# Raising VectorE's softmax bits in place: two passes per group of three score tiles instead of three, and 512-column GpSimd instructions

## The chip, the cores and the metric

The kernel runs on one core of one Trainium2 chip. The metric is the device time of one execution in microseconds (us). Five engines work side by side, each through its own instructions in order: TensorE (PE in the profile; PEld are its weight loads), VectorE (DVE), ScalarE (ACT), GpSimd (POOL) and SyncE (SP), which here only issues transfers. Times come from unprofiled runs; where the time goes is read from one profiled execution.

## The reference

Two attention blocks read the same x (2048 x 512, bfloat16; 32 heads of 16) and are mixed by a gate per row:

```python
x = A_x
g = _sigmoid((x * gate_w).sum(-1, keepdims=True))
a = _A_ref(x, A_wqkv, A_wo)      # full attention: softmax(q k^T / 4) v over all 2048 keys, 32 heads
b = _B_ref(x, B_wqkv, B_wo)      # each row attends to 8 rows: itself and 2, 4, ..., 14 rows back
return g * a + (1 - g) * b
```

Block A is the bulk: 32 heads x 2048 x 2048 exponentials. Block B has 8 scores per row and head.

## The kernel before

**Block A.** The 2048 queries are cut into 4 chunks of 512, the heads into 8 groups of four; the 32 pairs of chunk and head group are the *periods*. In a period there are 64 score tiles of 128 keys x 512 queries (16 key tiles x 4 heads). Most go this way: TensorE computes scores into one of two PSUM rings (three tiles and two tiles in turn), ScalarE takes one exponential of the whole ring (`pT<-ring`), and TensorE multiplies the result with the values (`vp_all`) into the period's accumulator.

**VectorE's groups.** Some score tiles (`n_dve`: 3 to 9 in the first eight periods, 12 in each later one, 339 in all) bypass ScalarE. They come in groups of `NGR` = 3 tiles, so there are 113 groups. `d_set` (L1220) lays out a group: TensorE computes each tile's scores (`dq`), and `p1` on VectorE turns them into a 16-bit integer, scale times score plus a constant, whose bits read as bfloat16 approximate the exponential. To make this better, the same bits are also used raised by 1, 2 and 3 times `STEP` = 32, and the four versions (steps 0 to 3, `NV` = 4) are multiplied with the values under four weights (`vp_all`, and `vd_all`, which holds the values times `WEIGHTS`) and added up in the accumulator. The raised copies are made by `sh` (L1263): three VectorE passes per group, each from the group's buffer `dt` into a buffer of its own, `pd`. A pass reads 1536 elements per partition as six runs of 256 and writes three rows of 512 that lie `ROW` = 514 apart. The matmuls of a step are `dpv` (L1276): three matmuls, one per tile. From period `LATE0` = 8 on, the weights of block A are no longer needed and two of the three `dt` buffers lie in their memory (`wkv`); there are three `pd` buffers (`NPD`).

**Block B.** The 16 tiles of 128 rows of block B run beside it (`b_tile`, L882): projections on TensorE, evacuated by VectorE and written to DRAM; SyncE loads the shifted rows back (`ksh`, `vsh`); GpSimd multiplies, adds up and normalises (`prod`, `av`, `lg`), adds the two last parts into `obb`, and TensorE transposes that for the output projection (`fin`). Most of GpSimd's instructions work on `HB` = 256 columns, so a row of 512 takes two. Partial sums of `av` are made by transfers that GpSimd issues (`av_sum`), for the last two tiles by GpSimd itself. GpSimd also normalises block A's periods (`po2a`, `po2b`).

**Order.** Nothing in the order is left to the chip. Every piece of work is an `op` with an engine, an estimated duration (`parts`), a due time and dependencies; `list_schedule` (L175) simulates the engines and writes down, for each engine, the order in which its instructions are issued. Resources such as buffers and PSUM banks are tokens. A part of a duration that is marked as shared (`True` in `parts`, as in `GP` for GpSimd and `SB` for two kinds of VectorE passes) takes its turn on one common `port` in that simulation. The three `sh` passes are not marked as shared. Due times of block B come from `b_start` and `b_space` (us from one tile to the next); those of the groups from `tn`, the planned time of the score set beside which a tile was placed: the raises at tn + 1.5 + 2(m - 1), their matmuls at tn + 4.5 + 2m.

Of the kernel before, what the change touches and what calls it, by code (L numbers as in the profile page):

```python
# [22 lines left out]
    b_space=(44.0,) * 4 + (47.0,) * 4 + (49.0,) * 8,  # L23
# [16 lines left out]
ROW = QW + 2  # L40
# [3 lines left out]
NPD = 3  # L44
NDE = 1
NDL = 3
# [5 lines left out]
def _ap(base, dims):  # L52
    return bass.AP(tensor=base.tensor, offset=base.offset, ap=[list(d) for d in dims])
# [47 lines left out]
POOL_G, NPG = (), 1  # L101
# [5 lines left out]
SB = lambda n: [(True, 0.065 + n / 3840.0)]  # L107
TT = lambda n: [(True, 0.075 + n / 960.0)]
# [9 lines left out]
P1D, SHD, PO1D = -100.0, 2.0, 300.0  # L118
# [183 lines left out]
def kernel(  # L302
# [75 lines left out]
    def mm_k(out, c, i, rhs, start, stop):  # L378
        for j in range(4):
            w = wkv[:, c, (4 * i + j) * DH:(4 * i + j + 2) * DH] if j < 3 else wk3[:, c, i, :, :].rearrange("p e d -> p (e d)")  # L380
            mm(out[32 * j:32 * j + 32, :], w, rhs, start, stop, tile_position=(0, 32 * j))
# [77 lines left out]
    wkv = const.tile([128, DC, 2 * D], BF16, name="wkv")  # L459
    wq = const.tile([128, DC, D], BF16, name="wq")  # L460
    wq2 = const.tile([128, DC, 8, 2, DH], BF16, name="wq2")
    q_scr = tc.dram_tile([NG * NC // 2 * 16, DH * QW], BF16, name="q_scr")
    wk3 = const.tile([128, DC, NG, 2, DH], BF16, name="wk3")
# [25 lines left out]
    dt_a = const.tile([128, NDE * NGR * QW], BF16, name="dt_a")  # L489
    pd_a = const.tile([128, (NPD + NPG) * NGR * ROW], BF16, name="pd_a")  # L490
    wkv_l = wkv[:].rearrange("p c n -> p (c n)")
    dt_bufs = [dt_a[:, k_ * NGR * QW:(k_ + 1) * NGR * QW] for k_ in range(NDE)]
    dt_bufs += [wkv_l[:, k_ * NGR * QW:(k_ + 1) * NGR * QW] for k_ in range(NDL - NDE)]
    pd_bufs = [pd_a[:, k_ * NGR * ROW:(k_ + 1) * NGR * ROW].rearrange("p (q n) -> p q n", q=NGR) for k_ in range(NPD + NPG)]
# [58 lines left out]
    def load_w(part):  # L553
        def s():
            out = wkv[:, :, (part - 1) * D:part * D] if part else wq[:]
            SP.dma_start(out=out, in_=a_w3[:, :, part * D:(part + 1) * D])
        return s
# [16 lines left out]
    xtok = [tok("gat", NGA) if sc < NGA else tok("pd", NPD) for sc in range(NC)]  # L574
# [13 lines left out]
    def k3(E, i0, i1):  # L588
        def s():
            wk = wkv[:, :, 0:D].rearrange("p c (i j d) -> p c i j d", i=NG, j=4)  # L590
            for e, j in ((0, 3), (1, 0)):
                E.tensor_copy(out=wk3[:, :, i0:i1, e, :], in_=wk[:, :, i0:i1, j, :])
        return s
# [113 lines left out]
    def v_proj(h0, h1, tb, TB, tag, dl, rel=0.0):  # L707
# [4 lines left out]
        def mk(half):  # L712
            def s():
                if half == 0:
                    st["pv"] = misc_ps([128, TB, n], tag=tag)
                for tt in range(half * TB // 2, (half + 1) * TB // 2):
                    t = tb + tt
                    for c in range(DC):
                        mm(st["pv"][:, tt, :], xT[:, c, t * 128:(t + 1) * 128],
                           wkv[:, c, D + h0 * DH:D + h1 * DH], c == 0, c == DC - 1)  # L720
            return s
# [158 lines left out]
    HB = D // 2  # L880

    def b_tile(t):  # L882
# [195 lines left out]
        for g_, (hf, wp) in enumerate(halves):  # L1078
            ps_ = mulp(logits_mul, hf, wp) + [logits_add(hf, wp, *x) for x in adds] + [logits_out(hf, wp)]
            srcs = [None] * nm + [1, 3] + list(range(nm + 1, nm + na - 1))  # L1080
            lgs.append([(g_, k_, p_, srcs[k_], ([lk[hf], qa] if k_ == 0 else [])) for k_, p_ in enumerate(ps_)])
        lseq = lgs[0][:nm]
        for g_ in range(len(halves)):
            nxt = lgs[g_ + 1][:nm] if g_ + 1 < len(halves) else []
            ad = lgs[g_][nm:]
            lseq += ad[:3] + nxt[:2] + ad[3:] + nxt[2:]
# [28 lines left out]
        b = op("pool", 0.0, av_last(0), tb + 43, deps=[a1], alloc=[tbb], use=[tav], name=f"B{t}", parts=GP("ff", HB))  # L1115
        a1 = op("pool", 0.0, av_last(HB), tb + 43, deps=[a1], after=[b], use=[tav, tbb], name=f"B{t}", parts=GP("ff", HB))
# [99 lines left out]
    wkv_users = [o for o in ops if o.eng == "pe" and o.name.startswith(("kp", "vp"))]  # L1216
    d_st, d_last, d_sh = {}, [None, None], []
    d_count, d_ends, d_sg = [0, 0, 0, 0], [], []

    def d_set(pi, gi, t, j, qk_, tn):  # L1220
# [5 lines left out]
        if first:  # L1226
            slot = d_count[0] % NDL if late else d_count[2] % NDE
            d_count[0] += late
            d_count[2] += not late
            d_st[key] = dict(dt=dt_bufs[slot], td=tok("dtl", NDL) if late else tok("dt", NDE), js=[], ts=[], p1=[])  # L1230
# [17 lines left out]
        if first and late and d_count[0] <= NDL:  # L1248
            deps += wkv_users + d_ends[-NV * NDE:]
# [10 lines left out]
        def on_pool(m):  # L1260
            return m == NV - 1 and gi in POOL_G

        def sh(m, pb):  # L1263
            def s():
                o_, i_ = pb.bitcast(U16)[:, :, 0:QW], g["dt"].bitcast(U16)
                i_ = _ap(i_, [list(i_.ap[0]), [QW // 2, 2 * NGR], [1, QW // 2]])
                (G if on_pool(m) else V).tensor_scalar(out=o_, in0=i_, scalar1=STEP * m, scalar2=None, op0=ALU.add)
            return s

        def pv(m, pb):  # L1270
            def s():
                for n1, (t_, j_) in enumerate(zip(g["ts"], g["js"])):
                    pv_mm(pi, t_, j_, pb[:, n1, 0:QW], vd_all[:, m - 1, t_ - (NT - NTD)] if m else vp_all[:, t_])
            return s

        def dpv(m, pb, deps, use, dl):  # L1276
            b = op("pe", 0.0, pv(m, pb), dl, mode="c", js=g["js"], full=1, deps=deps + [o_t0[pi]] + vs,
                   use=[use, acc_tok[pi]], name=f"dpv{pi}")
            o_pv[pi].append(b)
            d_ends.append(b)  # L1280
        dpv(0, g["dt"].rearrange("p (q n) -> p q n", q=NGR), list(g["p1"]), g["td"], tn + 4.5)
        for m in range(1, NV):
            if on_pool(m):
                pb = pd_bufs[NPD + d_count[3] % NPG]
                d_count[3] += 1
                tp = tok("pg", NPG)
                a = op("pool", 0.0, sh(m, pb), GFIRST, deps=list(g["p1"]), alloc=[tp], use=[g["td"]], name=f"sg{pi}",
                       after=d_sg[-1:], parts=GP("one", NGR * QW))
                d_sg.append(a)
            else:  # L1290
                pb = pd_bufs[d_count[1] % NPD]
                d_count[1] += 1
                tp = tok("pd", NPD)
                a = op("dve", 0.0, sh(m, pb), tn + 1.5 + SHD * (m - 1), deps=list(g["p1"]), alloc=[tp], use=[g["td"]],
                       lat=0.065 + NGR * QW / 1920.0 + SH_LAT, after=d_sh[-1:],
                       parts=[(False, 0.065 + NGR * QW / 1920.0)], name=f"sh{pi}")
                d_sh.append(a)
            dpv(m, pb, [a], tp, tn + 4.5 + SHD * m)
# [200 lines left out]
```

## Time and profile before

| what | us |
|---|---|
| three runs: lowest, median, highest | 814.36, 819.31, 820.49 |
| the profiled execution's own time | 815.66 |
| its span, first to last instruction | 813.9 |
| ScalarE busy | 785.7 |
| first exponential starts, last one ends | 19.58, 805.1 |
| VectorE's raising passes, 339 in all | 175.3 + 135.3 |
| GpSimd busy | 633.8 |
| last `obb` ends, its transposes start | 775.5, 790.43 |

The span in 40 slices of about 20 us (tenths of a slice that an engine is busy):

```profile
PE   8999999999999998999889999989989999898996
...
DVE  5646776897887999989989899997988899898887
ACT  2999999999999999999999999999999999999995
POOL 3098969799899999999997794989769419899910
```

A group line of the profile gives line, engine, operation, output <- input, shapes and count, then busy time in us and the mean duration of one in ns, then the idle time of the engine just before these instructions and what ended it. A line of a timeline gives start, duration, engine, what it is and how many are merged. The line L364 is the helper through which VectorE, ScalarE, GpSimd and SyncE issue everything, L373 the same for TensorE, so groups are told apart by tile names: `pd_a<-dt_a` and `pd_a<-wkv` are the raising passes, `dt_a<-misc_ps` and `wkv<-misc_ps` the `p1` passes.

### The profile page before, as it was taken

The page shows a single profiled execution, that of the slowest core. Times are in us where ns is not written, and L with a number is a line of the kernel's source. Part 1 is how long each engine was busy: PE and PEld are TensorE (multiplying, and loading weights), DVE is VectorE, ACT ScalarE, POOL GpSimd, SP SyncE. Part 2 cuts the span into 40 slices and gives each one's busy share as a digit, 9 for nine tenths or more (in the row PEclk, how much of TensorE's full clock was granted, in tenths as well). Part 3 has the DMA queues.
Part 4 walks back from the last instruction along what each step waited for, and adds up shares of the span by engine and source line. Part 5 has one row for each costly group of instructions (what it writes and reads, how often), then busy time and mean ns, then how long its engine had stood idle before and what let it go on. Part 6 is the DMA issues. An engine that isn't in the chain of part 4 may idle for free.

```text
span 813.9 us, 18012 instructions
## 1 busy us (share of the span) xinstructions
PE 751.9 (92%) x6962; PEld 246.2 (30%) x7018; DVE 690.2 (85%) x1080; ACT 785.7 (97%) x706; POOL 633.8 (78%) x1058
## 2 busy tenths in 40 slices
PE   8999999999999998999889999989989999898996
PEld 4333334324222222222222222323222222222322
DVE  5646776897887999989989899997988899898887
ACT  2999999999999999999999999999999999999995
POOL 3098969799899999999997794989769419899910
PEclk9999999999999999999999999999999999999998
DMA  7503071533544344443524407162440521522000
GB/s 261 143 2 118 2 172 50 135 86 100 132 118 112 95 114 131 103 127 93 149 55 119 126 17 171 45 162 54 91 125 12 124 92 49 147 59 72 1 2 27
DMA packets 58886, 77.22 MB, mean 95 GB/s; under 512 B 3744, under 2 KB 50848, under 8 KB 58800
## 3 DMA queue, kind: packets, MB, share of 16 engines
q1 hardware_dynamic: 52752, 54.05, 21.5%
q0 software_dynamic: 6048, 22.02, 14.6%
q8 instruction: 55, 0.90, 0.5%
q14 instruction: 31, 0.25, 0.1%
HBM read 43.78 MB, written 10.26 MB: 66 GB/s over the span
## 4 chain that ended last, share of the span: by engine, by line
ACT 46%; PE 28%; issue 18%; POOL 4%; DVE 3%; DMA 1%; SPq 0%; DVEq 0%; ACTq 0%
ACT pT L364 46%; PE misc_ps L373 19%; PE ring L373 8%; POOL prod L364 2%; POOL av L364 1%; DMA xld<-in_A_x_dram 1%; DVE kt_all L364 1%; ACT lg L364 1%; DVE pd_a L364 1%; PE pxt L622 0%; DVE wkv L364 0%; DVE osb L364 0%; POOL lg L364 0%; POOL obb L364 0%; DVE accT L364 0%
## 5 line engine op out<-in xcount | busy, mean ns | idle before, releaser
L364 ACT ACTIVATE pT<-ring 128x1536 bf16<-128x1536 f32 (+1 forms) x684 | 778.6, 1319 | 10.3 <-PE ring L373 9.8
L373 PE MATMUL ring<-qt,kt_all 32*128 32x512 bf16 x1709 | 270.4, 382 | 46.1 <-ACT pT L364 36.7
L364 POOL TENSOR_TENSOR prod<-ksh,qb 128x256 f32<-128x256 bf16 x256 | 175.8, 745 | 65.2 <-DMA ksh<-kv_scr 32.8
L373 PE MATMUL misc_ps<-pT,vp_all 128*17 128x512 bf16 (+1 forms) x1709 | 208.6, 383 | 0.1
L373 PEld LDWEIGHTS <-kt_all 32*128 32x128 bf16 x2048 | 88.4, 91 | 299.7 <-issue 290.4
L364 DVE TENSOR_SCALAR pd_a<-wkv 128x1536 uint16<-128x1536 uint16 x192 | 175.3, 941 | 1.7 <-PE misc_ps L373 0.6
L364 POOL TENSOR_TENSOR prod<-prod 128x256 f32<-128x256 f32 (+1 forms) x256 | 167.1, 668 | 5.8
L364 DVE TENSOR_SCALAR wkv<-misc_ps 128x512 uint16<-128x512 f32 x192 | 129.2, 683 | 27.9 <-PE misc_ps L373 23.1
L373 PE MATMUL misc_ps<-z 128*32 128x512 bf16 x421 | 138.9, 386 | 1.6 <-DVE z L364 1.6
L364 DVE TENSOR_SCALAR pd_a<-dt_a 128x1536 uint16<-128x1536 uint16 x147 | 135.3, 944 | 1.0
L373 PE MATMUL misc_ps<-pd_a,vd_all 128*17 128x512 bf16 x1017 | 131.3, 381 | 0.2
L373 PE MATMUL misc_ps<-qt,kt_all 32*128 32x512 bf16 x339 | 125.2, 380 | 2.4 <-DVE wkv L364 0.7
L364 DVE TENSOR_SCALAR dt_a<-misc_ps 128x512 uint16<-128x512 f32 x147 | 99.1, 685 | 18.3 <-PE misc_ps L373 16.9
L364 POOL TENSOR_TENSOR prod<-vsh,lg 128x256 f32<-128x256 bf16 x128 | 81.7, 739 | 0.0
L364 POOL TENSOR_TENSOR av<-vsh,lg 128x256 f32<-128x256 bf16 x128 | 79.6, 657 | 0.0
L373 PEld LDWEIGHTS <-vp_all 128*17 128x17 bf16 (+1 forms) x2048 | 54.7, 88 | 80.1 <-issue 66.2
L373 PE MATMUL misc_ps<-bw,xT 128*128 128x512 bf16 x164 | 50.8, 384 | 2.6 <-issue 1.1
L373 PEld LDWEIGHTS <-z 128*32 128x32 bf16 x421 | 37.0, 96 | 50.7 <-issue 28.1
L373 PEld LDWEIGHTS <-vd_all 128*17 128x17 bf16 x1017 | 35.1, 88 | 47.6 <-issue 38.0
L373 PEld LDWEIGHTS <-xT 128*128 128x128 bf16 x576 | 30.2, 99 | 33.4 <-issue 29.2
L364 POOL DMA_DIRECT2D av<-av x14 | 12.3, 882 | 33.3 <-DMA av<-prod 33.3
L373 PE MATMUL misc_ps<-xT,wkv 128*32 128x512 bf16 x384 | 37.9, 382 | 0.0
(89 smaller groups left out, 584.2 us busy)
## 6 DMA issues: line engine op xcount, KB each, us to landing
ksh<-kv_scr SPq DMA_DIRECT2D x32, 512.0 KB
vsh<-kv_scr SPq DMA_DIRECT2D x32, 512.0 KB
av<-prod POOLq DMA_DIRECT2D x28, 512.0 KB, 5.8
av<-av POOLq DMA_DIRECT2D x14, 512.0 KB, 5.0
kv_scr<-kvs SPq DMA_DIRECT2D x16, 256.0 KB
qt<-q_scr SPq DMA_DIRECT2D x30, 128.0 KB
out_dram<-osb SPq DMA_DIRECT2D x16, 128.0 KB
q_scr<-qs SPq DMA_DIRECT2D x15, 128.0 KB
```

The source lines that it names most:

```text
L364: return chain_on(key, f(*a, **k))
L373: return chain(nc.tensor.matmul(out, lhsT=lhsT, rhs=rhs, start=start, stop=stop, **kw))
```

## The change

A group's buffer becomes 3072 elements wide (`ROWB` = 2 x 3 x 512). `p1` fills its first half as before. Then there are two passes, both in place and over one contiguous run, instead of three into buffers of their own: `raise1` writes the first half plus `STEP` into the second half (1536 elements), and `raise2` adds 2 x `STEP` to the whole buffer (3072 elements). Steps 0 and 1 are multiplied between the two passes, steps 2 and 3 after the second, which therefore waits for the matmuls of steps 0 and 1.

In the simulation the two passes are marked as shared (`PT`). The `pd` buffers go. There are two wide buffers (`NDT`) in the first eight periods and two more (`NCB`) from period 8 on, in the memory of A's weights: K weights, V weights, `wq2` and `wk3` now lie in one tile `wall` of 2 x 3072 elements. `HB` becomes 512: GpSimd's multiplies and the first level of its additions work on 512 columns, and `obb` is written by one instruction. Block B's tiles are due at closer intervals (`b_space`). An option to make raised copies on GpSimd, unused before (`POOL_G` was empty), is removed.

```diff
-    b_space=(44.0,) * 4 + (47.0,) * 4 + (49.0,) * 8,
+    b_space=(43.0,) * 4 + (45.0,) * 4 + (47.0,) * 8,
...
-ROW = QW + 2
-NPD = 3
-NDE = 1
-NDL = 3
+NDT = 2
+NCB = 2
+ROWB = 2 * NGR * QW
...
+PT = lambda n: [(True, 0.1 + n / 3840.0)]
...
-P1D, SHD, PO1D = -100.0, 2.0, 300.0
+P1D, SH1, SH2, PO1D = -100.0, 1.5, 4.0, 300.0
+DP = (3.0, 3.5, 6.0, 6.5)
...
+    wall = const.tile([128, NCB * ROWB], BF16, name="wall")
+    wkw, wvw = (wall[:, k_ * DC * D:(k_ + 1) * DC * D].rearrange("p (c n) -> p c n", c=DC) for k_ in range(2))
...
+    pd_a = const.tile([128, NDT * ROWB], BF16, name="pd_a")
+    cb_bufs = [b_[:, k_ * ROWB:(k_ + 1) * ROWB] for b_, n_ in ((pd_a, NDT), (wall, NCB)) for k_ in range(n_)]
...
-    HB = D // 2
+    HB = D
...
-            lseq += ad[:3] + nxt[:2] + ad[3:] + nxt[2:]
+            lseq += ad[:1] + nxt[:1] + ad[1:2] + nxt[1:] + ad[2:]
...
-        b = op("pool", 0.0, av_last(0), tb + 43, deps=[a1], alloc=[tbb], use=[tav], name=f"B{t}", parts=GP("ff", HB))
-        a1 = op("pool", 0.0, av_last(HB), tb + 43, deps=[a1], after=[b], use=[tav, tbb], name=f"B{t}", parts=GP("ff", HB))
+        a1 = op("pool", 0.0, av_last(0), tb + 43, deps=[a1], alloc=[tbb], use=[tav], name=f"B{t}", parts=GP("ff", HB))
...
-    wkv_users = [o for o in ops if o.eng == "pe" and o.name.startswith(("kp", "vp"))]
+    wkv_users = [o for o in ops if o.eng == "pe" and (o.name.startswith(("kp", "vp")) or o.name in ("qp0", "qp1"))]
...
+        n_w = NGR * QW
+        flat = g["dt"].bitcast(U16)
+
+        def raise1():
+            V.tensor_scalar(out=flat[:, n_w:2 * n_w], in0=flat[:, 0:n_w], scalar1=STEP, scalar2=None, op0=ALU.add)
+
+        def raise2():
+            V.tensor_scalar(out=flat, in0=flat, scalar1=2 * STEP, scalar2=None, op0=ALU.add)
+
+        def pv(m):
...
+                    c0 = (m % 2 * NGR + n1) * QW
+                    pv_mm(pi, t_, j_, g["dt"][:, c0:c0 + QW], vd_all[:, m - 1, t_ - (NT - NTD)] if m else vp_all[:, t_])
...
+        a = op("dve", 0.0, raise1, tn + SH1, deps=list(g["p1"]), use=[g["td"]], after=d_sh[-1:], lat=0.0,
+               parts=PT(n_w), name=f"sh{pi}")
+        d_sh.append(a)
+        a.lat = a.occ + LAT["dve"] + SH_LAT
+        b = [dpv(0, list(g["p1"]), tn + DP[0]), dpv(1, [a], tn + DP[1])]
+        a = op("dve", 0.0, raise2, tn + SH2, deps=b, use=[g["td"]], after=d_sh[-1:], lat=0.0, parts=PT(2 * n_w),
+               name=f"sh{pi}")
+        d_sh.append(a)
+        a.lat = a.occ + LAT["dve"] + SH_LAT
+        dpv(2, [a], tn + DP[2])
+        dpv(3, [a], tn + DP[3])
```

The three removed `sh` passes with their `dpv` matmuls, and the old buffers, stand in the kernel before (L1260 to L1298 and L489 to L494).

## The prediction

> **What bounds the kernel now.** I read the page's busy times and costliest groups first, then busy time by stretch, then ScalarE's waits.
>
> ```profile
> PE 751.9 (92%) x6962; PEld 246.2 (30%) x7018; DVE 690.2 (85%) x1080; ACT 785.7 (97%) x706; POOL 633.8 (78%) x1058
> ...
> L364 ACT ACTIVATE pT<-ring 128x1536 bf16<-128x1536 f32 (+1 forms) x684 | 778.6, 1319 | 10.3 <-PE ring L373 9.8
> ...
> L364 DVE TENSOR_SCALAR pd_a<-wkv 128x1536 uint16<-128x1536 uint16 x192 | 175.3, 941 | 1.7 <-PE misc_ps L373 0.6
> ```
> ```profile
> 200.00:400.00 200.00, 187.73 (x1607) 57.42 (x1623) 183.76 (x274) 199.11 (x180) 187.84 (x316) 1.00 0.46 115
> 400.00:700.00 300.00, 278.52 (x2426) 84.19 (x2441) 272.86 (x400) 300.00 (x271) 227.75 (x385) 1.00 0.37 94
> ```
> ```profile
> ACT pT L364 <- PE ring L373: 9.8, 11, 5.1
> ```
>
> The stretches list PE, weight loads, DVE, ACT, POOL, clock, DMA. ScalarE's exponentials set the end: from the first (19.58 us) to the end of the last (805.1) ScalarE is idle only 10.3 - 5.1 = 5.2 us (the 5.1 lies ahead of the first). The change leaves all 684 alone, so it can win only those 5.2 us, what little hides between the records, and the tail of 8.8 us. In 400 to 700 us 265 of ScalarE's 271 instructions are exponentials: 132.5 pairs (five score tiles each), 2.264 us a pair; the fastest pairs of the timeline start 2.235 apart. It can lose wherever it makes TensorE late for a ring. VectorE (92% in 200 to 400) and TensorE (94%) have little room, and GpSimd (94%) none while it catches up.
>
> The next rows show a raise's new partner, GpSimd. Fills of kt_all and the mask of qa are the passes of before that read one even, contiguous run from SBUF to SBUF, as the raises will; today's raising pass splits its output into three rows.
>
> ```profile
> 72.56 1.28 DVE L364 TENSOR_SCALAR kt_all<-kt_all,rowc,negk 128x2048 bf16<-128x2048 bf16 x1
> ```
> ```profile
> 72.63 1.75 POOL L364 TENSOR_TENSOR prod<-ksh,qb 128x256 f32<-128x256 bf16 x2
> ```
> ```profile
> 208.44 0.80 DVE L364 TENSOR_SCALAR kt_all<-kt_all,rowc,negk 128x2048 bf16<-128x2048 bf16 x1
> ```
> ```profile
> 152.07 2.89 DVE L364 TENSOR_SCALAR kt_all<-kt_all,rowc,negk 128x2048 bf16<-128x2048 bf16 x1
> ```
> ```profile
> L364 DVE TENSOR_SCALAR qa<-qs x15: 282/446/1175, 22.2 to 731.4; 128x256 uint32<-128x256 uint32 x15
> ...
> L364 DVE TENSOR_SCALAR pd_a<-dt_a x147: 886/944/955, 35.1 to 797.7; 128x1536 uint16<-128x1536 uint16 x147
> ```
>
> The fill takes 0.80 us with GpSimd idle (208.44) and 1.28 beside it (72.56), where two GpSimd multiplies took 1.75 us; elsewhere two such take 1.29 to 1.30. So each lost about 0.46 us to the other. At 152.07 the fill stood through a run of four multiplies, 2.09 us. Today's raise (886 to 955 ns) takes no notice of GpSimd.
>
> **The raises.** There are 339/3 = 113 groups. Removed: three passes each, 113 x 2.67 us (three in a row take 2.67 in the timeline at 180.43). Added: one pass over 1536 and one over 3072 elements. The fills alone give (0.803 - 0.407)/(2048 - 512) = 0.258 ns per element; the fixed part is 0.944 - 1536 x 0.52 = 0.145 us for an immediate operand, 0.275 for the fills' per-partition ones. That makes 0.54 + 0.94 = 1.48 us a group (at most 1.74). Taken: 1.5, as the raise has an immediate. To it come two waits for GpSimd. From 39.8 us on, 21 fills and masks took 0.32 us longer than alone on average, beside instructions of 256 columns (0.63 us from start to start). With 512 columns an instruction lasts some 1.11 us, so I scale the wait to 0.55; bounds 0 and 1.1. A group costs VectorE 1.5 + 1.1 = 2.6 us: as good as the 2.67 of now. VectorE gains nothing.
>
> **GpSimd.** Joined into 512 columns: 128 pairs of K products, 128 of V, 64 of additions, 16 of obb, 12 of the last tiles' sums: 348. A row of 128 columns takes 427 ns and one of 256 748, so 0.11 us is fixed; the timeline's pitches make it 0.14. At 0.125, 348 x 0.125 = 43 us go, 2.7 per tile of B. Against this a pass costs GpSimd 0.46/2048 per element: 0.35 + 0.69 = 1.04 us a group where they meet. Tiles 3 to 7 of B ended (obb) at 259.4 and 417.0: 39.4 us each with GpSimd 94% busy, its rate flat out. A period has 64 - 12 = 52 exponentials' tiles, 52/5 x 2.264 = 23.6 us for four groups, 5.9 a group. So a tile takes (39.4 - 2.7)/(1 - 1.04/5.9) = 44.6 us, and the last obb, 12 tiles after the fourth, ends at 259.4 + 12 x 44.6 = 795 instead of 775.5. Its transposes stand at 790.43 and their chain (evacuation, output matmuls, a copy) ends at 797.7, 11 us before the final addition at 808.72: obb may come as late as 801. Cost: 0, covered by 6 us; every us beyond is lost.
>
> [...]
>
> **Raises into TensorE.** Pairing each pass with its matmuls in the timeline, half of them start within 0.7 us of the pass's end, a quarter within 0.4; half the exponentials start within 0.37 us of their last ring matmul's end, of which 0.11 can't be saved. So a raise that GpSimd holds a microsecond longer than the written order assumes blocks TensorE's queue, where the next ring stands. What it costs isn't in the trace; the nearest rows are the nine fills and masks held over 0.3 us (39.77, 72.56, 112.40, 122.23, 152.07, 210.62, 312.34, 434.69, 684.20). Within 4 us behind them ScalarE is idle 0.23 (before 42.65), 0.43 (113.25) and 0.23 (316.09): 0.89/9 = 0.10 us each. Of 226 raises I take 60% held over 0.3 us (0.81 of 1.11 us of an instruction, at nine tenths and somewhat less for the short ones): 226 x 0.6 x 0.10 = 13.6 us. Bounds: 0, if the order has room; 34, if half of them wait 0.55 us against a cover of 0.25.
>
> New in VectorE's queue: the second raise waits for the matmuls of step 0 and 1, and behind it stand the evacuations of the next scores, for whose banks TensorE waits. Today all three passes need only the finished scores. Cover: VectorE's idle time, 16 of 200 us, 0.5 us a group. Taken at 0.
>
> **The rest.** The tail ends today with six raises in 5.24 us (799.71), ahead of the last matmuls; two groups without GpSimd take 3.0. But the last exponential ends at 805.13, so -0.5 at most; taken. Weights in one tile: the same transfers in longer runs, 0; if they were slower, the first exponential would move by as much. Raising in place holds a buffer until the fourth step's matmul; two early and four late buffers stand against 5.9 us a group: 0. Earlier due times for B move its loads up in SP's queue, but GpSimd works in order and lags its due times: 0; covered by its 32.8 us of waits for ksh.
>
> **The sum.** The profiled execution took 815.66 us, 1.76 over its span; the three runs lie 1.3 below to 4.8 above (median 819.31). 815.66 + 13.6 - 0.5 = 828.8, and something for GpSimd's thin cover: 830, slower. Its own range is 828 to 842.
>
> **Rivals.** *No change:* the written order has room. For it: the fill at 152.07 stood 2.09 us too long and ScalarE ran on (four exponentials in 4.99 us from 153.16). Against: fills have no TensorE waiter at hand. 815.66 + 0 to 10: 820. Here belongs the case that the raises don't run at the fill's rate: at 0.52 ns, 0.94 + 1.74 = 2.68 us a group and no meeting with GpSimd, so no change either.
> *Faster:* early groups (ScalarE's idle lies before 320 us) find VectorE freer, as GpSimd is idler there; its 5.2 us go, half of the (2.264 - 2.235) x 341 = 10 us between pairs not owed to B's 16 exponentials (about 5), and the tail's 0.5: 815.66 - 8 = 808. It decides if the waits stay under (2.67 - 1.5)/2 = 0.58 us. Against: 0.55 expected.
> *GpSimd becomes the bound:* it decides above (801 - 259.4)/12 = 45.1 us a tile, half a us over my value. At 1.3 us lost per group a tile takes 47.1, the last obb comes at 824.6, 24 late: 839. If passes hold GpSimd for their whole 1.48 us, 49.0, 46 late: 862. For: 94% busy in 200 to 400. Against: the 0.46.
>
> **Chances.** Forecast 0.38, GpSimd 0.14, no change 0.38, faster 0.10. One per cent is about what a measurement here can tell from none: 811.1 to 827.5 around 819.31. So faster 0.10, same 0.38, slower 0.52. The range 811 to 848 leaves out the faster case and about two thirds of the GpSimd one.
>
> **What would show it.** Raises near 0.54 and 0.94 us with GpSimd idle and about 0.5 more beside it; GpSimd's products at 1.1 us, some 0.35 to 0.7 longer beside raises; ScalarE idle 15 to 20 us, behind TensorE's ring, late in the span too. No further idle time would refute the forecast; a last obb after 801 speaks for GpSimd; raises without waits for the faster case.

## The result, and the profile after

The changed kernel took 843.76 us (median of 4 runs, 839.46 to 849.45), the kernel before 817.77 beside it: a ratio of 1.033 (95% interval 1.030 to 1.037), so about 26 us slower. That is inside the forecast's range (811 to 848) and just above its own range (828 to 842); the direction was right, the size too small.

The profiled execution took 844.3 us with a span of 842.5. The page's busy times, the clock in 40 slices and three group lines:

```profile
PE 763.5 (91%) x6947; PEld 243.6 (29%) x7000; DVE 668.4 (79%) x967; ACT 789.7 (94%) x706; POOL 669.4 (79%) x710
...
PEclk9999999998999899999999999999999999999998
...
L364 ACT ACTIVATE pT<-ring 128x1536 bf16<-128x1536 f32 (+1 forms) x684 | 782.0, 1289 | 35.2 <-PE ring L373 28.2
...
L364 DVE TENSOR_SCALAR pd_a<-pd_a 128x1536 uint16<-128x1536 uint16 (+1 forms) x130 | 153.4, 1180 | 15.3 <-PE misc_ps L373 14.2
...
L364 DVE TENSOR_SCALAR wall<-wall 128x1536 uint16<-128x1536 uint16 x96 | 121.5, 1271 | 16.8 <-PE misc_ps L373 16.2
```

The column that moved is ScalarE's idle time: 35.2 us ahead of the same 684 exponentials (10.3 before). The first exponential starts at 19.54 us (19.58 before) and the last ends at 833.99 (805.13), with 8.54 us behind it (8.76): nothing came in ahead of the stream, 0.2 us was won behind it, and the whole loss lies in it. Added up from the start of one activation to that of the next, less the shortest such distance for its shape, ScalarE is 45.0 us late in this execution and was 16.2 late before: 28.8 us more. Some 11 us of that fall between 200 and 300 us and 17 between 300 and 700; ahead of 200 us the two kernels are as late as each other, and behind 700 they differ by 1 us. The two raises take 153.4 + 121.5 = 274.9 us, where the three passes took 310.6.

Busy time by stretch (PE, weight loads, DVE, ACT, POOL, granted clock, DMA) and ScalarE's waits (total, times, longest):

```profile
200.00:400.00 200.00, 178.07 (x1458) 51.59 (x1470) 163.20 (x213) 188.57 (x168) 168.90 (x178) 0.97 0.40 102
400.00:700.00 300.00, 272.07 (x2307) 80.14 (x2320) 253.03 (x336) 288.02 (x258) 269.94 (x282) 0.99 0.36 92
```
```profile
ACT pT L364 <- PE ring L373: 28.2, 36, 5.1
...
ACT pT L364 <- PE misc_ps L373: 5.7, 4, 2.2
```

ScalarE was busy for all of 400 to 700 before; now 12 us are missing there, and no other engine is full: TensorE 272 of 300, VectorE 253, GpSimd 270. Engines with room and a late stream mean waits in a row, not a new bound. TensorE's waits name the first of them (in the kernel before, this view gave `wkv` 1.0 us, `dt_a` 0.2 and `pd_a` none):

```profile
PE misc_ps L373 <- DVE pd_a L364: 11.7, 17, 1.5
PE misc_ps L373 <- DVE wall L364: 11.3, 16, 2.0
```

So 23.0 us of TensorE's time stand behind VectorE's group buffers, in 33 waits. One such wait, from the timeline of the changed kernel (start, duration, engine; in brackets the idle time ahead of the instruction):

```profile
101.13 1.05 POOL L364 DMA_DIRECT2D av<-prod  x1
101.74 3.46 DVE L364 TENSOR_SCALAR pd_a<-pd_a 128x3072 uint16<-128x3072 uint16 x1 [0.28 <-PE misc_ps L373]
101.94 2.43 POOL L364 TENSOR_TENSOR prod<-vsh,lg 128x512 f32<-128x512 bf16 x2
105.25 0.39 PE L373 MATMUL misc_ps<-pd_a,vd_all 128*17 128x512 bf16 x3 [1.51 <-DVE pd_a L364]
108.36 2.36 ACT L364 ACTIVATE pT<-ring 128x1536 bf16<-128x1536 f32 x2 [3.18 <-PE ring L373]
```

A second raise, 0.95 us alone, takes 3.46. It ends 0.8 us after GpSimd's two multiplies do (104.37), about a raise's own length: it did not wait for one instruction of GpSimd only, but for the whole run behind the transfer that GpSimd had just issued. TensorE stands, and ScalarE's next ring is 3.18 us late. Of all 226 raises, 120 waited over 0.3 us and 14 over 1.5, and all 14 of these began 0.35 to 1.5 us after the start of a transfer issued by GpSimd (`av<-prod` or `av<-av`). The other way round, 23 raises began within 1.5 us of such a start: 16 of them were held 1.3 us or more and 7 not at all. Of the 203 others none was held over 1.2 us, though 132 of them came in or just ahead of a run of two or more GpSimd instructions without a gap. So it is not a run alone that goes with the long stands, but one behind a transfer. So far that is a coincidence in time; the experiments test it.

### The profile page after: what moved, and what is told of

It reads as the page before. It is cut to its first block, busy times and chain, and to the rows that moved or that the text cites. A ratio compares the mean times of both kernels' runs of the same rounds, so it can differ in the third digit from the quotient of the medians.

```text
span 842.5 us, 17539 instructions
## 1 busy us (share of the span) xinstructions
PE 763.5 (91%) x6947; PEld 243.6 (29%) x7000; DVE 668.4 (79%) x967; ACT 789.7 (94%) x706; POOL 669.4 (79%) x710
## 4 chain that ended last, share of the span: by engine, by line
ACT 38%; PE 29%; issue 17%; DVE 14%; DMA 1%; ACTq 0%; SPq 0%; DVEq 0%
ACT pT L364 37%; PE misc_ps L373 20%; PE ring L373 8%; DVE pd_a L364 6%; DVE wall L364 6%; DMA xld<-in_A_x_dram 1%; DVE qa L364 1%; DVE kvs L364 0%; PE pxt L621 0%; DVE kt_all L364 0%; DVE vd_all L364 0%; DVE qs L364 0%; DVE vp_all L364 0%; ACT lg L364 0%; DVE qb L364 0%
## 5 line engine op out<-in xcount | busy, mean ns | idle before, releaser
L364 ACT ACTIVATE pT<-ring 128x1536 bf16<-128x1536 f32 (+1 forms) x684 | 782.0, 1289 | 35.2 <-PE ring L373 28.2
L364 POOL TENSOR_TENSOR prod<-ksh,qb 128x512 f32<-128x512 bf16 x128 | 170.9, 1364 | 41.4 <-DMA ksh<-kv_scr 34.0
L364 POOL TENSOR_TENSOR prod<-prod 128x512 f32<-128x512 f32 (+2 forms) x192 | 187.6, 977 | 3.2
L364 DVE TENSOR_SCALAR pd_a<-pd_a 128x1536 uint16<-128x1536 uint16 (+1 forms) x130 | 153.4, 1180 | 15.3 <-PE misc_ps L373 14.2
L364 DVE TENSOR_SCALAR pd_a<-misc_ps 128x512 uint16<-128x512 f32 x195 | 130.6, 680 | 39.7 <-PE misc_ps L373 36.8
L364 DVE TENSOR_SCALAR wall<-wall 128x1536 uint16<-128x1536 uint16 x96 | 121.5, 1271 | 16.8 <-PE misc_ps L373 16.2
L364 DVE TENSOR_SCALAR wall<-misc_ps 128x512 uint16<-128x512 f32 x144 | 95.4, 682 | 17.4 <-PE misc_ps L373 13.5
L364 POOL TENSOR_TENSOR prod<-vsh,lg 128x512 f32<-128x512 bf16 x64 | 80.8, 1326 | 0.0
L373 PE MATMUL misc_ps<-pd_a,vd_all 128*17 128x512 bf16 x585 | 73.1, 384 | 7.3 <-DVE pd_a L364 7.1
L364 POOL TENSOR_TENSOR av<-vsh,lg 128x512 f32<-128x512 bf16 x64 | 79.4, 1269 | 0.1
L373 PE MATMUL misc_ps<-wall,vd_all 128*17 128x512 bf16 x432 | 54.5, 386 | 9.7 <-DVE wall L364 9.5
```

The lines of the kernel that those rows point to most:

```text
L364: return chain_on(key, f(*a, **k))
L373: return chain(nc.tensor.matmul(out, lhsT=lhsT, rhs=rhs, start=start, stop=stop, **kw))
```

## Experiments

Ratios are to the kernel before, timed beside each (margin's row leaves out its run of 878.13 us). "Late" is ScalarE's lateness as worked out above (16.2 before, 45.0 after), good to about 1 us. "At half clock" is the time inside the stream of the profiled execution in which TensorE's granted clock was 0.50; in all of these runs it came in stretches of 3.41 us and multiples of it (four of 3.41 and one of 6.83 in the changed kernel).

| kernel | median us | ratio (95%) | raises held over 1.5 us | at half clock, us | late, us |
|---|---|---|---|---|---|
| before | 817 | 1 | 0 | 3.4 | 16.2 |
| after | 843.76 | 1.033 (1.030 to 1.037) | 14 | 20.5 | 45.0 |
| pool512 | 818.67 | 1.003 (1.002 to 1.005) | 0 | 3.4 | 19.2 |
| no_products | 817.57 | 1.000 (0.998 to 1.002) | 0 | 0 | 17.2 |
| fast_copies | 866.23 | 1.060 (1.057 to 1.064) | 16 | 64.9 | 66.8 |
| wait_only | 844.54 | 1.032 (1.027 to 1.038) | 0 | 30.7 | 35.8 |
| raise256 | 860.71 | 1.053 (1.050 to 1.055) | 15 | 30.7 | 43.8 |
| margin | 870.3 | 1.064 (1.058 to 1.071) | 6 | 68.3 | 62.6 |
| two_buffers | 850.39 | 1.038 (1.031 to 1.044) | 11 | 44.4 | 55.7 |
| drain | 823.42 | 1.007 (1.004 to 1.010) | 0 | 0 | 23.9 |
| drain2 | 823.23 | 1.008 (1.006 to 1.011) | 0 | 0 | 22.6 |
| drain_ahead | 844.88 | 1.034 (1.028 to 1.040) | 13 | 17.1 | 42.9 |

**The parts of the change alone.** *pool512* is the kernel before with GpSimd's part only (`HB = D` and what follows from it).

> The kernel before with GpSimd's 512 columns alone (order planned anew): raising passes as before. Theories A and B: ScalarE still sets the end and GpSimd gains 40 us that nothing waits for, 811 to 820 us. Theory C (512 columns cost the time, by longer instructions): 825 us or more.

GpSimd falls from 633.8 to 582.0 us busy and the time stays, to 0.3%. The wider instructions alone win nothing here, where GpSimd is not late, and lose little (19.2 us late instead of 16.2).

*fast_copies* is the kernel before with its three passes made contiguous: the same order of work, but passes that meet GpSimd.

```diff
-ROW = QW + 2
+ROW = QW
...
-                i_ = _ap(i_, [list(i_.ap[0]), [QW // 2, 2 * NGR], [1, QW // 2]])
+                i_ = i_.rearrange("p (q n) -> p q n", q=NGR)
```

> The kernel before with its own order on every engine; only the three raising passes of a group read and write three even rows without a gap on both sides, so that they should run in the form of the fills. Own buffers stay, so no pass waits for a matmul. Theory A (a pass that meets GpSimd has no fixed duration, and the written order of TensorE leaves no room for that): passes of 0.55 us alone, some 0.85 us on average beside GpSimd, TensorE waits more than 10 us in all for raised copies, 830 to 850 us. Theory B (the second raise in place waits for the matmuls of steps 0 and 1, a round trip through TensorE): nothing waits here, so 812 to 820 us. Theory C (512-column instructions on GpSimd cost the time): they are not in this kernel, 812 to 820 us.

The groups of the passes (shortest/median/longest in ns) in the profile of fast_copies:

```profile
L364 DVE TENSOR_SCALAR pd_a<-wkv x192: 496/749/4685, 254.8 to 853.6; 128x1536 uint16<-128x1536 uint16 x192
L364 DVE TENSOR_SCALAR pd_a<-dt_a x147: 497/789/4777, 34.9 to 848.1; 128x1536 uint16<-128x1536 uint16 x147
```

Most passes became faster (median 0.77 us, before a steady 0.94), some took almost five times as long, and the kernel lost 49 us without any raise in place. GpSimd pays too: 711.9 us busy against 633.8, and its last `obb` ends at 836.

*wait_only* is the kernel before with the slow, steady passes and with the change's wait: step 2's copy overwrites step 1's buffer and so waits for the matmuls of steps 0 and 1, at the due times of the change.

```diff
+SHT = (0.0, 1.5, 4.0, 4.0)
+DP = (3.0, 3.5, 6.0, 6.5)
...
+                new = m != 2
+                a = op("dve", 0.0, sh(m, pb), tn + SHT[m], deps=list(g["p1"]) + (bs[:2] if m > 1 else []),
+                       alloc=[tp] if new else [], use=[g["td"]] + ([] if new else [tp]),
```

> The kernel before with its slow passes that take no notice of GpSimd, but step 2's copy is written over step 1's buffer, so that the second and third passes stand in VectorE's queue until the matmuls of step 1 are done, with the due times of the changed kernel for passes and matmuls. Theory A: 815 to 825 us. Theory B: the round trip is all here, 832 to 845 us. Theory C: 815 to 820 us.

It lost 27 us too, though no pass was held. VectorE's waits show where: it stood ahead of the copies, for the matmuls.

```profile
DVE pd_a L366 <- PE misc_ps L375: 27.3, 39, 2.7
```

This kernel has an order of its own (the planner laid it out anew for passes of 2.8 us a group), so it does not price the wait in the changed kernel. The next one does.

*no_products* is the changed kernel, in its own order, with block B's products, their sums and the last sums on 32 of 512 columns; what it leaves out is the rest of block B's work on GpSimd, so that block B's result is not complete. The transfers that GpSimd issues carry 32 columns as well.

```diff
-                G.tensor_tensor(out=st["prod", hf, wp][:, w_, c0:c0 + HB], in0=st["ksh", hf][:, wp + w_, c0:c0 + HB],
-                                in1=st["qb"][:, c0:c0 + HB], op=ALU.mult)
+                G.tensor_tensor(out=st["prod", hf, wp][:, w_, c0:c0 + CW], in0=st["ksh", hf][:, wp + w_, c0:c0 + CW],
+                                in1=st["qb"][:, c0:c0 + CW], op=ALU.mult)
```

> The changed kernel with its own order, but GpSimd's products, additions and sums for block B work on 32 of 512 columns: left out is the rest of block B, so GpSimd is mostly idle. Raises and their waits for matmuls stay as they are. Theory A: raises take 0.55 and 0.95 us with little spread, ScalarE's idle time falls back to 5 to 8 us, 810 to 822 us. Theory B: 835 to 845 us, as the round trip is untouched. Theory C: like A, 810 to 822 us.

The raises in the profile of no_products:

```profile
L364 DVE TENSOR_SCALAR pd_a<-pd_a x130: 495/897/1219, 34.8 to 797.4; 128x1536 uint16<-128x1536 uint16 x65, 128x3072 uint16<-128x3072 uint16 x65
L364 DVE TENSOR_SCALAR wall<-wall x96: 496/918/1002, 261.4 to 802.6; 128x1536 uint16<-128x1536 uint16 x48, 128x3072 uint16<-128x3072 uint16 x48
```

0.575 and 0.962 us on average, none long, and the kernel is as fast as the one before. The second raise's wait for matmuls is there and costs nothing, though VectorE has more room here than in the change (559 us busy instead of 668): what costs is meeting GpSimd. VectorE's saved time (559 us busy instead of 690) buys nothing either, as the forecast said.

*two_buffers* gives the second raise a buffer of its own, so that it waits for no matmul (one of two output buffers makes room).

```diff
-            V.tensor_scalar(out=flat, in0=flat, scalar1=2 * STEP, scalar2=None, op0=ALU.add)
+            V.tensor_scalar(out=pr.bitcast(U16), in0=flat, scalar1=2 * STEP, scalar2=None, op0=ALU.add)
...
-        a = op("dve", 0.0, raise2, tn + SH2, deps=b, use=[g["td"]], after=d_sh[-1:], lat=0.0, parts=PT(2 * n_w),
+        a = op("dve", 0.0, raise2, tn + SH2, deps=[a], alloc=[tr], use=[g["td"]], after=d_sh[-1:], lat=0.0, parts=PT(2 * n_w),
```

> The changed kernel with the second raise written into a buffer of its own (3072 wide), so that it waits for no matmul; passes keep their size and form, GpSimd its 512 columns (order planned anew; one output buffer less). Theory A (passes meet GpSimd): 832 to 846 us, as they still do. Theory B (the round trip through TensorE, which cost 26 us with the slow passes): 815 to 825 us.

Eleven raises were still held over 1.5 us, and it is no faster than the change, in an order of its own. Removing the wait wins nothing that can be seen.

*raise256* is the change without GpSimd's part (`HB = D // 2`).

> The changed kernel with GpSimd's instructions at 256 columns as before (order planned anew). Theory A: a pass waits for half an instruction, so the mean wait falls from 0.47 to some 0.3 us, and the loss of 26 us by about a third: 830 to 840 us, unless GpSimd, with 43 us more to do, comes late for its last tile. Theory B: 840 to 846 us. Theory C: 815 to 825 us.

Here the GpSimd rival of the forecast is to be seen. The stream ends at 832.9, as in the changed kernel, but 25 us follow, and TensorE's waits have a line that none had so far:

```profile
PE misc_ps L1126 <- POOL obb L364: 7.5, 2, 7.2
```

GpSimd is 726.6 us busy and its last `obb` ends at 849.6. Raises that meet GpSimd need the wider instructions: they are worth 17 us inside the change (860.71 - 843.76) and nothing outside it.

**More slack in the order.** *margin* plans each raise to be ready 0.7 us later (`SH_LAT` 1.0 instead of 0.3).

> The changed kernel, planned with 0.7 us more between the end of a raise and its matmuls (SH_LAT 1.0 instead of 0.3), so that TensorE's queue holds other work there. If the loss comes from TensorE standing before raised copies that are late (theory A), its 23 us of waits for VectorE's raised copies fall under 10 us and the time to 826 to 838 us. If the loss comes from something that a raise does not wait for (GpSimd's share, theory C), it stays at 838 to 850 us.

```profile
PE misc_ps L373 <- DVE pd_a L364: 25.2, 44, 1.9
PE misc_ps L373 <- DVE wall L364: 3.2, 6, 0.9
```

These two lines of TensorE's waits were to shrink from 23.0 us to under 10 and add up to 28.4; the kernel is some 26 us slower than the change. The planner's new order stands in more places than the slack helps.

**The stands behind transfers.** *drain* puts a memset and two one-element copies, each reading what the one ahead wrote, behind every transfer that GpSimd issues (its expectation names the 28 from `prod`; they stood behind all 42).

```diff
                     G.dma_start(out=av[:, wp:wp + WP, :], in_=st["av", wp][:], accum_op=ALU.add)
+                G.memset(drn[:, 0:1], 0.0)
+                G.tensor_copy(out=drn[:, 1:2], in_=drn[:, 0:1])
+                G.tensor_copy(out=drn[:, 0:1], in_=drn[:, 1:2])
```

> The changed kernel with three tiny dependent GpSimd instructions behind each transfer that adds prod into av (28 transfers; order otherwise as it is). In the changed kernel every raise that stood over 1.5 us started within some 1.5 us of a transfer issued by GpSimd and stood until GpSimd's run of instructions behind it had its next wait. If that run, which leaves VectorE no gap, is what holds them (theory A2), stands over 2 us go from 8 to 3 or fewer and the time falls by 5 to 12 us, to 831 to 839 us, though GpSimd has some 15 us more to do. If the long stands have another reason, they stay, and the time is 842 to 850 us.

*drain_ahead* has the same three instructions ahead of each transfer instead.

> Control to the kernel with tiny dependent instructions behind GpSimd's transfers: the same three instructions, as often, but ahead of each transfer. If it is the run of GpSimd instructions right behind a transfer that shuts VectorE out (theory A2), the raises that stand over 2 us remain (5 or more of 226) and the time stays at 836 to 850 us. If the tiny instructions help in another way (by spacing GpSimd's work, or by giving VectorE gaps anywhere), it falls to 820 to 830 us here too.

*drain2* has only the memset and one copy behind it.

> The changed kernel with two tiny instructions behind each transfer instead of three (a fill and one copy that waits for it): one wait of GpSimd for itself. Theory A2: one such wait ends the run behind the transfer as well as two, stands over 2 us 2 or fewer, 818 to 828 us. If it takes two, some stands stay and the time is 828 to 842 us.

Behind the transfer the added work takes 20 us off the kernel; ahead of it, the same work leaves the time at 844.88, with 13 raises held over 1.5 us. The place counts, not the work. The timeline of drain2 at the place shown above:

```profile
101.14 1.65 POOL L364 DMA_DIRECT2D av<-prod  x1
101.74 0.96 DVE L364 TENSOR_SCALAR pd_a<-pd_a 128x3072 uint16<-128x3072 uint16 x1 [0.28 <-PE misc_ps L373]
101.91 1.00 POOL L364 MEMSET drn<- 128x1 f32 x1
102.98 0.19 POOL L364 COPY drn<-drn 128x1 f32<-128x1 f32 x1
103.13 2.15 POOL L364 TENSOR_TENSOR prod<-vsh,lg 128x512 f32<-128x512 bf16 x2
106.55 3.71 ACT L364 ACTIVATE pT<-ring 128x1536 bf16<-128x1536 f32 x3 [1.37 <-PE ring L373]
```

The same raise starts at the same time and takes 0.96 us instead of 3.46; now it is GpSimd's transfer and memset that are stretched, to 1.65 and 1.00 us (0.87 and 0.40 at the next transfer, 105.59). The copy's wait for the memset is not what let VectorE in here: the raise is over at 102.70, and the copy starts at 102.98. In drain2, 19 raises began within 1.5 us of the start of a transfer; 18 of them took no more than some 0.1 us longer than alone, and 13 of these were over before the copy began. What helps is thus at least in part that a memset stands behind the transfer where a multiply stood. No run has the memset alone, or a small instruction of another kind, so which property of the pair does it is not shown. TensorE's waits for the group buffers fall from 23.0 us to 4.4 in drain:

```profile
PE misc_ps L373 <- DVE wall L364: 2.3, 7, 0.6
PE misc_ps L373 <- DVE pd_a L364: 2.1, 7, 0.6
```

The ordinary waits stay: 103 raises of drain2 are held over 0.3 us, and it is 6.4 us later than before (22.6 - 16.2).

*fast_copies_drain* puts drain's three instructions into fast_copies.

> The kernel before with its own order and the three raising passes in the fast form (866 us), and the tiny dependent instructions behind each transfer that GpSimd issues. Theory A2: stands over 2 us go from 14 to 2 or fewer and most of the loss of 49 us goes, 820 to 840 us. If ordinary waits for one GpSimd instruction are what costs (theory A as predicted), it stays at 850 to 866 us.

879.75 us (1.076; 1.070 to 1.082): slower, not faster. No pass is held over 1.2 us any more, but GpSimd, with 256 columns and added work, is 736.8 us busy, and the transposes of `obb` start within about 1 us of its end in 13 of 16 tiles: GpSimd sets the pace, and 73% of the chain that ends last is GpSimd. That run says nothing against the stands: its bound is another.

**Why few stands cost so much.** The granted clock of the changed kernel around 205 us (PE, weight loads, DVE, ACT, POOL, clock, DMA):

```profile
200.00:204.00 4.00, 3.58 (x43) 1.69 (x41) 4.00 (x4) 3.22 (x3) 3.92 (x6) 1.00 0.60 115
204.00:208.00 4.00, 2.98 (x16) 0.48 (x15) 3.97 (x7) 1.41 (x2) 4.00 (x5) 0.72 0.11 20
208.00:212.00 4.00, 3.67 (x22) 0.86 (x23) 0.79 (x2) 2.36 (x2) 3.92 (x5) 0.50 0.01 2
212.00:216.00 4.00, 4.00 (x36) 1.01 (x33) 3.37 (x4) 3.85 (x4) 4.00 (x4) 0.93 0.12 33
```

A fill of kt_all that took 3.00 us behind a transfer at 200.28 made a raise late, TensorE stood (1.22 us in all from 202.3 to 205.7), and from 205.7 to 212.6 its clock was granted at one half: 16 and 22 matmuls in 4 us, where the rows around have 43 and 36, and ScalarE busy for 1.41 and 2.36 of 4 us. The runs of one and the same program agree: the changed kernel's four took 839.46, 843.22, 844.30 and 849.45 us at mean granted clocks of 0.990, 0.988, 0.985 and 0.973.

How much standing went with it can be counted. In each profiled execution all half-clock stretches of the stream begin on one grid of 3.41 us (the five of the changed kernel at 205.72, 280.81, 291.05, 567.53 and 618.73). The profiled executions of all 20 kernels, cut along their grids, have 4524 such windows at full clock. In 67 of them TensorE stood 1.6 us or more in all, and behind every one the clock was halved; with 1.0 to 1.6 us of standing it was halved behind 38 of 93, with less behind 20 of 4364. A stand that lies across two windows counts in parts.

To price it, three kernels repeat the first raise in 13 of the groups of drain2, whose profiled execution has no half clock in the stream: the result is the same, and VectorE is held by a length that can be set.

```diff
+        n_again = 4 if len(d_sh) % 18 == 8 else 0
+
         def raise1():
-            V.tensor_scalar(out=flat[:, n_w:2 * n_w], in0=flat[:, 0:n_w], scalar1=STEP, scalar2=None, op0=ALU.add)
+            for _ in range(1 + n_again):
+                V.tensor_scalar(out=flat[:, n_w:2 * n_w], in0=flat[:, 0:n_w], scalar1=STEP, scalar2=None, op0=ALU.add)
```

> drain2 with the first raise written twice more, with the same result, in 13 of the 113 groups (every ninth): 13 delays of 1.1 us by the 0.55 us of a raise alone. A delay of the raise reaches TensorE less what the order keeps as a cover, some 0.4 us. Theory S (only the stand itself costs): 13 x 0.7 = +9 us over drain2's 823: 832, TensorE's clock full but for at most two windows of 3.4 us. Theory C (a stand of TensorE above some 1.5 us in one window of 3.41 us also halves its granted clock for the next such window): stands of 0.7 us are too short for that, so also about 832, at most three windows at half clock.

> The same with four repeats in the same 13 groups: delays of 2.2 us. Theory S: 13 x 1.8 = +23 us over drain2: 847, 14 us more than dose2. Theory C: the stand of 1.8 us is followed by 3.41 us at half clock in most of the 13 places; TensorE is 93% busy, so each costs about 1.5 us more: +40 us, 860 to 866, with 8 to 13 places at half clock in the profiled execution.

> The same with six repeats: delays of 3.3 us. Theory S: 13 x 2.9 = +38 us over drain2: 861, again 14 more than dose4. Theory C: the step from dose4 is 14 us for the stands and what a few longer half-clock stretches add: 875 to 890, 11 to 13 places at half clock.

| kernel | median us | step | ratio (95%) | places with half clock | at half clock, us |
|---|---|---|---|---|---|
| drain2 | 823.23 | | 1.008 (1.006 to 1.011) | 0 | 0 |
| dose2 | 841.52 | 18.3 | 1.030 (1.026 to 1.034) | 5 of 13 | 30.7 |
| dose4 | 880.28 | 38.8 | 1.077 (1.074 to 1.081) | 12 of 13 | 81.9 |
| dose6 | 912.36 | 32.1 | 1.117 (1.114 to 1.121) | 12 of 13 | 109.2 |

The steps are far from the equal 14 us of a cost by the stand alone. All three came out slower than either theory said, because a repeat beside GpSimd takes longer than 0.55 us (the five of dose4 took 4.1 us at 112 and 6.5 at 523); the comparison place by place is free of that. Counted from 1 us ahead of the repeats to 12 us behind them: in the 8 places of dose2 without half clock, TensorE's longest stands within the stream add up to 4.8 us and ScalarE is 4.6 us late there: one for one. In the 5 with it, 9.9 us of longest stands and 20.9 us late: 2.2 us more per place. In dose4 the 12 places have 39.4 and 65.8 (2.2 more each), in dose6 62.9 and 91.4 (2.4). With every stand over 0.3 us counted there, and not the longest alone, it is 1.7 to 2.0 us more. One place without and one with, first the timeline of dose2, then the timeline and the windows of dose4:

```profile
611.84 1.93 DVE L364 TENSOR_SCALAR wall<-wall 128x1536 uint16<-128x1536 uint16 x3
616.02 0.39 PE L373 MATMUL misc_ps<-wall,vd_all 128*17 128x512 bf16 x3 [1.27 <-DVE wall L364]
```
```profile
523.23 6.46 DVE L364 TENSOR_SCALAR pd_a<-pd_a 128x1536 uint16<-128x1536 uint16 x5
529.74 0.60 PE L373 MATMUL misc_ps<-pd_a,vd_all 128*17 128x512 bf16 x3 [5.32 <-DVE pd_a L364]
```
```profile
524.00:528.00 4.00, 0.43 (x6) 0.18 (x4) 3.90 (x4) 1.93 (x2) 4.00 (x4) 0.88 0.00 0
528.00:532.00 4.00, 2.03 (x6) 0.56 (x6) 3.72 (x5) 0.00 (x0) 2.65 (x2) 0.50 0.00 0
532.00:536.00 4.00, 4.00 (x34) 0.92 (x33) 2.67 (x5) 3.14 (x3) 0.41 (x1) 0.77 0.17 66
```

After the 1.27 us of standing TensorE's matmuls took 0.39 us (the median of the score matmuls of the changed kernel is 0.38); after the 5.32 they took 0.60.

**Using the time.** VectorE is 77% busy in drain2. *drain15* gives it a fifth group in each period from the ninth on (`n_dve` 15, block B's tiles closer by 1 to 2 us), with drain's instructions; *drain2_mix*, *mix_late* and *mix_half* do so in every fourth period from the ninth on, every third from the fifteenth on and every second from the fourteenth on, with drain2's.

> A version that may beat both: the changed kernel with the tiny instructions behind the transfers, and 15 instead of 12 score tiles per period on VectorE from period 8 on, with block B due a little closer (42, 44, 45 us). ScalarE loses 72 of its 1709 tiles, 72 x 0.45 = 32 us. If GpSimd and VectorE keep up, 795 to 808 us; if GpSimd, whose obb was only just in time, sets the end, 805 to 825 us.

> drain2 with five of VectorE's groups instead of four in every fourth period from the ninth on: six groups more, which take 6 x 1.36 = 8 us off ScalarE and put 6 x 9 x 0.216 = 12 us on TensorE (9 more matmuls a group), which has some 25 us of standing left in the stream. Theory S and C alike: 815 to 818 if the order finds room for them without TensorE standing; if not, stands and half-clock windows take more than the 8 us and it comes out above 823.

> drain2 with five of VectorE's groups in every third period from the fifteenth on (six groups more, as in drain2_mix, but none while the projections of block A still run; drain2_mix lost 6.8 us between 250 and 300 us, most of it in a stretch of 17 us at half clock there, and about 1 us in each 50 us later). If that stretch belongs to the early additional group: 6 x 1.36 = 8 us less on ScalarE than drain2's 823 and nothing given back: 814 to 818, no half-clock window in the later half. If additional groups make TensorE stand wherever they are put: 819 or more, with half-clock windows after 350 us.

> The same with five groups in every second period from the fourteenth on: ten groups more, 13.6 us less on ScalarE, 10 x 9 x 0.216 = 19 us more on TensorE, which in these periods is then as full as ScalarE. If the order still finds room: 810 to 814. If TensorE becomes the bound of these periods, each late ring is followed by others: 820 to 850 with several half-clock windows.

drain15 took 1041.12 us (1.274; 1.267 to 1.280) with 222 us at half clock. drain2_mix took 820.02 (1.004; 1.002 to 1.007), 3.2 less than drain2; mix_late 826.01 (1.011; 1.008 to 1.015), with its half clock at 203 and 275 to 285 us, long before its first additional group, so that guess about drain2_mix was wrong; mix_half 858.98 (1.050; 1.046 to 1.054), late from 700 us on. Each added group costs TensorE nine matmuls; ten and 24 groups more (mix_half, drain15) came out far slower than six (drain2_mix, mix_late). No version came out below the kernel before; drain2_mix, the nearest with the change in it, is 0.4% above.

## Why the prediction was right in its path and wrong in its size

*The durations: right.* The raises take 0.55 and 0.95 us where nothing meets them (no_products: 0.575 and 0.962 on average; forecast 0.54 and 0.94). The 0.52 ns an element from which the forecast took its fixed part of 0.145 us was an estimate that no run shows (the kernel before plans its passes with it, 1/1920 us at L1295); the two raises of no_products give 0.252 ns an element and a fixed part of 0.19 us. The wait for GpSimd is 0.47 us on average (105.9 us over 226; forecast 0.55), and 53% wait over 0.3 us (forecast 60%). VectorE's two passes a group, 2.44 us, come as near to the old 2.67 as said.

*GpSimd, the wider columns and the rest: right.* GpSimd is not the bound: its last `obb` ends at 787.0 (forecast 795, deadline 801), and each tile's transposes come 6 us or more after it. The tail won 0.2 us (forecast 0.5). The second raise's wait for matmuls, taken at 0, is 0 in no_products, and at most part of the 6.4 us that stay in drain2. The rival with GpSimd as the bound appears as soon as the wider instructions are taken away (raise256).

*The path: right.* Raises held by GpSimd block TensorE's queue (23.0 us of its waits), and ScalarE runs dry behind its rings (28.2 us, 9.8 before), from 200 to 700 us. The faster case and that of no change fall with it; no_products shows that no change would have been the outcome with most of GpSimd's work gone. But most of the loss comes onto this path in two ways that the forecast did not have.

*The size: wrong.* The term "raises into TensorE" was put at 226 x 0.6 x 0.10 = 13.6 us and measured 45.0 - 16.2 = 28.8. Two steps of it failed: the price of a wait, and the clock.

First, it gave every wait the length of one GpSimd instruction at most and the price of an ordinary wait. For ordinary waits that price was too high, if anything: drain2 has 103 raises held over 0.3 us and 6.4 us of lateness, 0.06 us each. The rest comes from a tail that the forecast had before its eyes. The fill at 152.07 of the profile before is such a stand, through four multiplies, and it began 1.0 us behind a transfer:

```profile
151.06 0.88 POOL L364 DMA_DIRECT2D av<-prod  x1 [0.30 <-POOL prod L364]
```

It was used only as evidence that stands do no harm, because ScalarE ran on behind a fill for which TensorE did not wait at once. Behind a raise TensorE does. drain and drain2 take the stands away and 20 of the 26 us with them; drain_ahead, with the three instructions of drain in another place, takes none. Of the 28.8 us of lateness 22.4 go in drain2, and with them all half clock in the stream.

Second, TensorE's granted clock was taken as given. The changed kernel has 20.5 us of its stream at half clock, in five stretches (3.4 us before). By the doses such a place costs 2.2 to 2.4 us beyond its longest stand. Five of them would cost 11 to 12 us, less some 2 for the one place of the kernel before: an estimate of 9 us of the 28.8 for the clock, which leaves some 13 of the 22.4 for the stands themselves. A straight line through the times and clocks of the changed kernel's four runs gives 836 us at full clock, 8 below the median; the like line for the kernel before gives 814, 3 below. That puts the clock's share nearer 5 us. Between 5 and 9 is as near as these runs come.

In both steps the runs went beyond what the forecast allowed for. An ordinary wait was 0.36 us on average and at most 1.2 away from transfers, beside GpSimd multiplies of 1.17 (median of `prod<-ksh,qb`); the stands, in which a raise took up to 3.46 us, went through several instructions of GpSimd in a row and so past the forecast's bound of one. As to the clock, behind 1.6 us or more of standing within a window of 3.41 us it was halved every time (67 of 67), behind 1.0 to 1.6 us in 38 of 93.

*Left open.* Why GpSimd's run behind a transfer leaves VectorE no gap, and why a memset and a small copy behind the transfer end that, is not settled; the records show the effect and the cure only. The stand of 1.89 us in dose6 that had no half clock behind it lies across two windows, 1.46 us in the one and 0.43 in the other. Why some windows with less than 1.0 us of standing had half clock behind them is open. The orders that the planner laid out anew (wait_only, raise256, margin, two_buffers and the kernels with added groups) differ in many places at once: that they stand elsewhere and fall to half clock is seen, which decision of the planner is at fault is not. The 6.4 us by which drain2 stays later are put down to ordinary waits because no_products, where GpSimd's work is small, has none of them; they were not taken apart further.

## What to carry to other kernels

Before a VectorE pass is made contiguous and so fast, look for what GpSimd does beside it and who waits for the pass: a slow pass that nothing disturbed (0.89 to 0.96 us, all 339) served this kernel better than one of 0.55 us that now and then takes 3. Price the tail of a wait, not its mean, when an engine as busy as TensorE here (91%) stands behind it, and read the granted clock of each stretch with the waits: here a place where TensorE's clock was halved behind the stand cost about 2 us more than the stand (1.7 to 2.4 by the doses). Where VectorE passes stand behind transfers that GpSimd issues, a memset and a one-element copy that reads it, put behind each transfer, are a cheap cure to try; here they won back 20 of 26 us.

## What the hardware showed unexpectedly

- Behind a transfer issued by GpSimd, VectorE's pass stood through whole runs of GpSimd's instructions (16 of the 23 raises of the changed kernel that began within 1.5 us of such a start were held 1.3 us or more): it took up to 3.46 us for a raise of 0.95 and 4.78 us for a pass of 0.55 (fast_copies). In the changed kernel, raises that began later than 1.5 us after a transfer's start were held 1.2 us at most, also within a run. A memset and one dependent copy behind each of the 42 transfers ended the long stands (no raise held over 1.2 us in drain2), and most raises there were over before the copy began.
- In the 20 profiled executions TensorE's clock was granted at one half, within the stream, in whole windows of 3.41 us: behind each of the 67 windows with 1.6 us or more of standing, behind 38 of 93 with 1.0 to 1.6 us, and behind 20 of 4364 with less. Matmuls that took 0.39 us at full clock took 0.60 in them (dose4, at 529.74).
- In wait_only, a VectorE multiply of 16 elements per partition (`rden<-rden,g_rw`, at 807.09) took 3.59 us beside GpSimd; in the kernel before it took 0.17 (at 788.81 and 806.85). So an instruction as small as this was held too. It stood until GpSimd's run of additions ended at 810.65, with no transfer of GpSimd in the 62 us ahead of it: this one stood behind a plain run.
